# Window attention and maxout FFN on one core: in chunk 1 the mask of head pair 1 becomes a product on VectorE instead of two matmuls, and that pair's value products stand one group of FFN products later

## The chip, the core and the metric

The kernel runs on one core of a Trainium2 chip. The metric is device time in microseconds (us) of one execution. The kernel before takes 177.5 us, the median of 3 runs (177.43 to 177.53).

A core has five engines, each with its own in-order list of instructions; they wait for each other through semaphores. TensorE (PE in the profile) multiplies matrices: it loads a weight block (PEld), streams the other operand past it and writes to PSUM, which has eight banks. VectorE (DVE) and ScalarE (ACT) read PSUM and write SBUF. GpSimd (POOL) works in SBUF only and here also starts the loads of the weights. SyncE's queue (SP) starts the other transfers.

## The reference, cut to what matters

```python
# q, k, v: (4 batches, 8 heads, 768 positions, 64); n_sink 4, window 128
scores = scale * np.matmul(q, k.transpose(0, 1, 3, 2))
rel = pos[:, None] - pos[None, :]
keep = (pos[None, :] < n_sink) | ((rel >= 0) & (rel < window))
a = softmax(np.where(keep, scores, -1e9))
x = np.matmul(a, v)                     # heads put side by side: (3072, 512)
h = np.maximum(np.maximum(x @ w1, x @ w2), x @ w3)      # (3072, 768)
out = h @ w_out                                          # (3072, 512)
```

Inputs and output are float32; the kernel multiplies in bf16 and sums in float32.

## The kernel before, in words

The 3072 tokens are cut into 12 chunks of 256 (three to a batch). Heads go in four pairs, 0 to 3. Every chunk passes through the same steps, each a small function; the order in which their calls are written is the order in which each engine meets its instructions. No scheduler changes it.

- `score(ci, p)`: for one head pair, products of keys and queries (line 287) into two banks named `st`, one for each head of the pair. The window needs four 128x128 blocks per head in a chunk that is not the first of its batch.
- The mask comes in one of two ways. With `premask(ci, p)` ahead of the score, TensorE writes an additive mask (0 or a large negative number) into the two banks, one 128x512 product of the identity and `addm` for each (line 269), and the scores are added onto it; it takes the two banks that early. Without it the scores overwrite the banks, and after the exponential `mask(ci, p)` multiplies both heads' weights by a 0/1 mask in one VectorE instruction of 128x1024 (line 341).
- `expo(ci, p)`: the exponential on ScalarE, one instruction per head (line 335), from `st` to `e_sb`. It sets the two banks free.
- `sink_score` and `av_open`: scores of the four sink positions (line 349), their exponential (line 355), and then the first products into four banks named `o`, one per pair (line 381).
- `av(ci, p)`: the value products of one pair, eight in a chunk like chunk 1 (line 398, output `o`). VectorE then takes the reciprocal of the sums (line 403) and writes the normalised rows to `x_sb` (line 406), which frees the pair's `o` bank.
- `xpose(ci, t, nc.vector)`: four transposes on TensorE into a bank `xt` (line 419) and a copy on VectorE to `xT` (line 420), for each half t of the chunk.
- `ffn_h(ci, fp, wi)`: eight products of `xT` with two of the six column blocks of weight wi (line 438) into one bank `h_ps`. For wi = 0 ScalarE copies the result to `h_sb` (line 445); for wi = 1 and 2 VectorE takes the maximum of it and `h_sb` (line 449). Each of the eight products reads both halves of `xT`.
- `ffn_y(ci, t)`: the output products and their copy.

Banks are handed out from a list, first freed, first given, in the order in which the calls are written. So a call that takes banks earlier or later also changes which bank later calls get, and so for whom they wait.

The change lies in a prologue that is written out call by call, for chunks 0 to 3. Around it stand: scores of chunk 1, pair by pair (0, 2, 3, then 1); the first FFN group of chunk 0, `ffn_h(0, 2, 0)`; the value products of chunk 1; the other FFN groups of chunk 0; the transposes of chunk 1; and then the FFN groups of chunk 1, beginning with `ffn_h(1, 0, 0)`. The weights of the FFN come in parts while this runs, by loads from GpSimd's queue.

Of the kernel before, what the change touches and what calls it, by code (L numbers as in the profile page):

```python
# [16 lines left out]
def kernel(  # L17
# [31 lines left out]
    with tc.manual_schedule():  # L49
# [7 lines left out]
        def bank(shape, dtype, name):  # L57
            j = free.pop(0)
            x = psum.tile(shape, dtype, tag=f"b{j}", name=name)
            home[id(x)] = x, j  # L60
            return x

        def give(*banks):
            for x in banks:
                free.append(home.pop(id(x))[1])
# [10 lines left out]
        def load(ci, what="kqv", gate=None, part=None, parts=1):  # L76
            if ci >= NCH:
                return
            b, c = divmod(ci, CPB)
            t0 = c * 256  # L80
            for w in what:
                src = {"k": k, "q": q, "v": v}[w]
                if (ci, w) not in raws:
                    raws[ci, w] = raw.tile([128, H, 2, D], F32, tag=w + "_raw", name=w + "_raw")
                dst = raws[ci, w]
                if gate is not None:
                    gate(dst[0:1, 0, 0, 0:1])
                n = H // parts
                for g in range(parts) if part is None else (part,):
                    nc.sync.dma_start(  # L90
                        out=dst[:, n * g:n * g + n],
                        in_=src[b, n * g:n * g + n, t0:t0 + 256]
                            .rearrange("h (p i) d -> p h (i d)", i=2))
# [162 lines left out]
        def load_wo(a, b):  # L256
            nc.gpsimd.dma_start(out=wo[:, a:b],
                                in_=moe_w_out.rearrange("(a p) f -> p a f", p=128)[:, a:b])
# [5 lines left out]
        def premask(ci, pairs):  # L264
            lo = 0 if ci % CPB else 1
            for p in pairs:
                sts[ci, p] = [bank([128, 4, 128], F32, "st") for a in range(2)]
                for a in range(2):
                    nc.tensor.matmul(sts[ci, p][a][:, lo:], lhsT=ident, rhs=addm0 if lo else addm,  # L269
                                     start=True, stop=False, skip_group_check=True)  # L270
# [54 lines left out]
        def weight(ci, p, a, s):  # L325
            if (ci, 0) in packed:
                j, u = unit[p, s]
                return packed[ci, j][0][:, a, u]
            return es[ci, p][0][:, a, s]

        def expo(ci, p):
            lo = 0 if ci % CPB else 1
            e, st = es[ci, p]
            for a in range(2):
                nc.scalar.activation(e[:, a, lo:], st[a][:, lo:], AF.Exp, scale=scale)  # L335
                give(st[a])

        def mask(ci, p, eng=None):
            lo = 0 if ci % CPB else 1
            e = es[ci, p][0]  # L340
            (eng or nc.vector).tensor_mul(e[:, :, lo:], e[:, :, lo:], msk0 if lo else msk)  # L341

        def sink_score(ci):
            b, c = divmod(ci, CPB)
            if c == 0:
                return
            st = bank([128, 2, 128], F32, "sk")
            for p in range(NP):
                nc.tensor.matmul(  # L349
                    st[32 * p:32 * p + 32].rearrange("q n (i r) -> q n i r", i=2),  # L350
                    lhsT=ks[b % 2][:, p],
                    rhs=qT[ci % RING][:, p].rearrange("q i n r -> q n i r"),
                    start=True, stop=True, tile_position=(0, 32 * p))
            e = work.tile([128, 2, 128], BF16, tag="e_sink", bufs=2, name="e_sink")
            nc.scalar.activation(e, st, AF.Exp, scale=scale)  # L355
            give(st)
            es[ci, "sink"] = e
# [30 lines left out]
        def av(ci, p):  # L388
            b, c = divmod(ci, CPB)
            o = os_[ci, p]  # L390
            first = c == 0
            for t in range(2):
                for a in range(2):
                    blocks = [(1, ci, 0)] if t == 0 else [(2, ci, 0), (3, ci, 1)]
                    if t == 0 and c:
                        blocks = [(0, ci - 1, 1)] + blocks
                    for s, cv, n in blocks:
                        nc.tensor.matmul(  # L398
                            o[:, t, a], lhsT=weight(ci, p, a, s), rhs=vb[cv % RING][:, n, 2 * p + a],
                            start=first, stop=True, skip_group_check=True)  # L400
                        first = False
            rc = work.tile([128, 2, 2], F32, tag="rc", bufs=4, name="rc")
            nc.vector.reciprocal(rc, o[:, :, :, D])  # L403
            if ci not in xs:
                xs[ci] = work.tile([128, 2, NP, 2, D], BF16, tag="x", bufs=2, name="x_sb")
            nc.vector.tensor_mul(xs[ci][:, :, p], o[:, :, :, 0:D],  # L406
                                 rc.unsqueeze(3).to_broadcast([128, 2, 2, D]))
            give(o)
# [3 lines left out]
        def xpose(ci, t, eng=None):  # L412
            eng = eng or nc.scalar
            if ci not in xTs:
                xTs[ci] = work.tile([128, 2, DS, 128], BF16, tag="xT", bufs=3, name="xT")
            pt = bank([128, DS, 128], BF16, "xt")
            x = xs[ci][:, t].rearrange("q p a d -> q (p a d)")
            for ds in range(DS):
                nc.tensor.transpose(pt[:, ds], x[:, ds * 128:(ds + 1) * 128], ident)  # L419
            (nc.scalar.copy if eng is nc.scalar else eng.tensor_copy)(xTs[ci][:, t], pt)  # L420
            give(pt)
# [9 lines left out]
        def ffn_h(ci, fp, wi, cuts=1):  # L431
            if ci not in hs:
                hs[ci] = work.tile([128, FB, 256], BF16, tag="h", bufs=3, name="h_sb")
            hp = bank([128, 2, 256], F32, "h_ps")
            for f in range(2):
                c0 = (2 * fp + f) * 128
                for ds in range(DS):
                    nc.tensor.matmul(  # L438
                        hp[:, f].rearrange("q (i t r) -> q i t r", i=2, t=2),
                        lhsT=w_sb[wi][:, ds, c0:c0 + 128],  # L440
                        rhs=xTs[ci][:, :, ds].rearrange("q t (i r) -> q i t r", i=2),
                        start=(ds == 0), stop=(ds == DS - 1))
            dst = hs[ci][:, 2 * fp:2 * fp + 2]
            if wi == 0:
                nc.scalar.copy(dst, hp)  # L445
            else:
                for f in range(cuts):
                    x = slice(2 * f // cuts, 2 * (f + 1) // cuts)
                    nc.vector.tensor_max(dst[:, x], dst[:, x], hp[:, x])  # L449
            give(hp)  # L450
# [36 lines left out]
        def after(wi, c=0):  # L487

            def gate(dst):
                nc.gpsimd.tensor_copy(dst, w_sb[wi][0:1, 0, c:c + 1])  # L490
            return gate
# [78 lines left out]
        score(1, (3,))  # L570
        load_w(2, 512, 768)
        sink_score(1)
        premask(1, (1,))
        load(2, 'q', gate=pool_gate)
        cast_v(1, 1, 0, nc.gpsimd)
        load_w(2, 0, 256)
# [10 lines left out]
        av(1, 0)  # L587
        expo(1, 1)
        av(1, 3)
        av(1, 2)  # L590
        ffn_h(0, 1, 0)
        av(1, 1)
        ffn_h(0, 0, 0)
        load_wo(0, 3)
        xpose(1, 0, nc.vector)
        xpose(1, 1, nc.vector)
        load(3, 'k', gate=after(1))
        ffn_h(0, 2, 1)
        ffn_h(1, 0, 0)
        ffn_h(1, 2, 0)  # L600
        ffn_h(1, 1, 0)
# [341 lines left out]
```

## Time and profile before

| what | value |
|---|---|
| median of 3 runs | 177.5 us (177.43 to 177.53) |
| the profiled execution's own time | 177.67 us |
| span, first to last instruction, of that execution | 175.9 us |
| mean granted TensorE clock | 1.000 |
| DVE busy | 125.7 us (71%) |
| ACT busy | 86.0 us (49%) |
| POOL busy | 66.4 us (38%) |
| HBM read and written | 25.17 MB and 6.29 MB |

The span is what the trace shows; the time of the execution holds 1.77 us more that lie around it. Times in the trace count from the span's start. "Busy" of TensorE counts overlapping products once, and the end of a product is modelled: a 128x256 product is shown with 273 ns, though the next one starts 0.11 us after it. Starts are therefore the better measure of TensorE's pace. A bracket behind a row names the idle time just before it and what ended it; small waits carry none.

### The profile page before, as it was taken

How to read it: one execution, taken by the hardware profiler on the slowest of the kernel's cores; microseconds unless marked ns; L12 is line 12 of the kernel's file. 1: busy time of each engine (PE TensorE's matmuls, PEld its weight loads, DVE VectorE, ACT ScalarE, POOL GpSimd, SP SyncE). 2: the span in 40 equal slices, each digit the busy share in tenths (PEclk: the TensorE clock that was granted, in tenths of full speed). 3: DMA queues.
4: the chain of work that ended last, by engine and by line, in shares of the span. 5: the costliest groups of instructions: out<-in, count | busy, mean ns of one | idle time of the engine just before them, and what ended most of it. 6: DMA issues, size and time to landing. Idle time of an engine off the chain costs nothing.

```text
span 175.9 us, 4628 instructions
## 1 busy us (share of the span) xinstructions
PE 169.1 (96%) x1869; PEld 127.4 (72%) x1869; DVE 125.7 (71%) x267; ACT 86.0 (49%) x168; POOL 66.4 (38%) x128
## 2 busy tenths in 40 slices
PE   7789999999999999999999999999999999999991
PEld 2447889856896697697796796796895895896870
DVE  3499728697899687875875975977775875976550
ACT  3479831557847833914716815815517617510211
POOL 4799045146671828035525425326537000000000
PEclk9999999999999999999999999999999999999999
DMA  4999999999979496699999999999999429323203
GB/s 136 292 289 204 208 219 265 238 281 273 261 123 276 77 303 128 120 305 124 207 279 193 197 301 166 235 297 132 198 298 195 150 49 373 120 54 129 121 0 119
DMA packets 69573, 34.90 MB, mean 198 GB/s; under 512 B 26544, under 2 KB 68016, under 8 KB 69552
## 3 DMA queue, kind: packets, MB, share of 16 engines
q1 hardware_dynamic: 64912, 31.33, 78.5%
q0 software_dynamic: 4496, 3.15, 11.7%
q8 instruction: 14, 0.23, 0.6%
q10 hardware_dynamic: 144, 0.13, 0.2%
q14 instruction: 7, 0.06, 0.1%
HBM read 25.17 MB, written 6.29 MB: 179 GB/s over the span
## 4 chain that ended last, share of the span: by engine, by line
PE 91%; DMA 3%; DVE 3%; issue 0%; POOL 0%; ACT 0%; POOLq 0%
PE h_ps L438 54%; PE y_ps L459 18%; PE o L398 6%; PE st L287 6%; DMA q_raw<-in_q_dram 3%; DVE vb L108 2%; PE pt L118 1%; PE xt L419 1%; PE o L381 1%; PE sk L349 1%; PE st L307 1%; PE y_ps L469 1%; PE pt L140 1%; PE st L269 1%; DVE qT L122 0%; DVE k_bf L102 0%
## 5 line engine op out<-in xcount | busy, mean ns | idle before, releaser
L438 PE MATMUL h_ps<-xT,w 128*128 128x256 bf16 x864 | 100.7, 273 | 0.0
L438 PEld LDWEIGHTS <-w 128*128 128x128 bf16 x864 | 82.1, 98 | 10.1 <-issue 0.2
L449 DVE TENSOR_TENSOR h_sb<-h_sb,h_ps 128x512 bf16<-128x512 bf16 (+1 forms) x74 | 49.0, 670 | 18.7 <-PE h_ps L438 17.4
L445 ACT CAST h_sb<-h_ps 128x512 bf16<-128x512 f32 x36 | 21.2, 594 | 45.5 <-PE h_ps L438 45.5
L335 ACT ACTIVATE e_sb<-st 128x512 bf16<-128x512 f32 (+1 forms) x80 | 40.2, 594 | 3.3 <-PE st L287 2.0
L108 POOL CAST vb<-v_raw 64x512 bf16<-64x512 f32 x40 | 27.5, 688 | 13.5 <-DMA v_raw<-in_v_dram 12.1
L459 PE MATMUL y_ps<-wo,h_sb 128*128 128x512 bf16 x138 | 32.2, 380 | 0.0
L341 DVE TENSOR_TENSOR e_sb<-e_sb,msk 128x1024 bf16<-128x1024 bf16 (+1 forms) x34 | 25.1, 764 | 3.8 <-ACT e_sb L335 3.7
L102 POOL CAST k_bf<-k_raw 128x512 bf16<-128x512 f32 x19 | 11.2, 613 | 36.5 <-DMA k_raw<-in_k_dram 33.3
L459 PEld LDWEIGHTS <-h_sb 128*128 128x128 bf16 x138 | 12.5, 98 | 14.8 <-issue 1.2
L406 DVE TENSOR_TENSOR x_sb<-o,rc 128x256 bf16<-128x256 f32 x48 | 20.4, 424 | 1.7
L398 PE MATMUL o<-vb,e_sb 128*128 128x65 bf16 x352 | 16.7, 193 | 0.7 <-DVE vb L108 0.7
L398 PEld LDWEIGHTS <-e_sb 128*128 128x128 bf16 x352 | 14.9, 97 | 3.1 <-issue 0.7
L461 DVE COPY y_sb<-y_ps 128x512 f32<-128x512 f32 x12 | 8.3, 691 | 10.6 <-PE y_ps L459 10.5
L102 POOL CAST q_bf<-q_raw 128x512 bf16<-128x512 f32 x19 | 11.3, 617 | 9.5 <-DMA q_raw<-in_q_dram 9.3
L287 PE MATMUL st<-qT,kT 64*128 64x128 bf16 (+1 forms) x224 | 12.5, 237 | 0.5 <-DVE qT L122 0.5
L287 PEld LDWEIGHTS <-kT 64*128 64x128 bf16 x224 | 7.3, 94 | 5.8 <-issue 4.3
L403 DVE RECIPROCAL rc<-o 128x4 f32<-128x4 f32 x48 | 8.3, 174 | 3.5 <-PE o L398 3.4
L355 ACT ACTIVATE e_sink<-sk 128x256 bf16<-128x256 f32 x8 | 3.1, 390 | 14.2 <-PE sk L349 9.7
L318 ACT ACTIVATE e_sb<-st 128x512 bf16<-128x512 f32 x12 | 6.1, 615 | 4.7 <-PE st L307 4.7
L461 ACT COPY y_sb<-y_ps 128x512 f32<-128x512 f32 x11 | 6.5, 588 | 3.8 <-PE y_ps L459 3.4
L180 PE MATMUL warm<-wz 128*128 128x512 bf16 x11 | 4.9, 632 | 1.2 <-DVE wz L169 1.2
(77 smaller groups left out, 86.4 us busy)
## 6 DMA issues: line engine op xcount, KB each, us to landing
k_raw<-in_k_dram SPq DMA_DIRECT2D x12, 512.0 KB, 6.2
q_raw<-in_q_dram SPq DMA_DIRECT2D x12, 512.0 KB, 7.3
v_raw<-in_v_dram SPq DMA_DIRECT2D x12, 512.0 KB, 7.8
out_dram<-y_sb SPq DMA_DIRECT2D x11, 512.0 KB, 3.9
w<-in_moe_w_dram POOLq DMA_DIRECT2D x5, 256.0 KB, 8.1
w<-in_moe_w_dram POOLq DMA_DIRECT2D x2, 512.0 KB, 9.0
wo<-in_moe_w_out_dram POOLq DMA_DIRECT2D x2, 384.0 KB, 9.2
kT<-k_bf SPq DMA_TRANSPOSE x16, 3.4
```

The lines of the kernel that those rows point to most:

```text
L102: f(x[:, 2 * g:2 * g + 2].rearrange("q p i a d -> q p a i d"), y[:, 4 * g:4 * g + 4].rearrange("q (p a) i d -> q p a i d", a=2))
L108: (eng.copy if eng is nc.scalar else eng.tensor_copy)(vb[ci % RING][64 * i:64 * i + 64, n, :, 0:D], raws[ci, "v"][64 * n:64 * n + 64, :, i])
L287: nc.tensor.matmul(st[a][:, s:s + q1 - q0].rearrange("q n (i r) -> q n i r", i=2), lhsT=x[hp, n, p].rearrange("q i r -> q (i r)"), rhs=qc[ ...
L335: nc.scalar.activation(e[:, a, lo:], st[a][:, lo:], AF.Exp, scale=scale)
L341: (eng or nc.vector).tensor_mul(e[:, :, lo:], e[:, :, lo:], msk0 if lo else msk)
L398: nc.tensor.matmul(o[:, t, a], lhsT=weight(ci, p, a, s), rhs=vb[cv % RING][:, n, 2 * p + a], start=first, stop=True, skip_group_check=True)
L406: nc.vector.tensor_mul(xs[ci][:, :, p], o[:, :, :, 0:D], rc.unsqueeze(3).to_broadcast([128, 2, 2, D]))
L438: nc.tensor.matmul(hp[:, f].rearrange("q (i t r) -> q i t r", i=2, t=2), lhsT=w_sb[wi][:, ds, c0:c0 + 128], rhs=xTs[ci][:, :, ds].rearrang ...
L445: nc.scalar.copy(dst, hp)
L449: nc.vector.tensor_max(dst[:, x], dst[:, x], hp[:, x])
L459: nc.tensor.matmul(yp, lhsT=hs[ci][:, fb, t * 128:(t + 1) * 128], rhs=wo[:, fb], start=(fb == 0), stop=(fb == FB - 1))
L461: (nc.scalar.copy if eng is None else eng.tensor_copy)(ys[ci][:, t], yp)
```

## The change

```diff
         score(1, (3,))
         load_w(2, 512, 768)
         sink_score(1)
-        premask(1, (1,))
         load(2, 'q', gate=pool_gate)
...
         ffn_h(0, 2, 0)
         score(1, (1,))
         av_open(1)
         av(1, 0)
         expo(1, 1)
         av(1, 3)
+        mask(1, 1)
         av(1, 2)
         ffn_h(0, 1, 0)
+        ffn_h(0, 0, 0)
         av(1, 1)
-        ffn_h(0, 0, 0)
         load_wo(0, 3)
+        ffn_h(0, 2, 1)
         xpose(1, 0, nc.vector)
         xpose(1, 1, nc.vector)
         load(3, 'k', gate=after(1))
-        ffn_h(0, 2, 1)
         ffn_h(1, 0, 0)
```

The additive mask of pair 1 is gone, and with it two 128x512 products; `score(1, 1)` now takes its two banks itself, behind `ffn_h(0, 2, 0)`, and its products start fresh instead of adding. One product on VectorE masks the weights after the exponential. `av(1, 1)` changes places with `ffn_h(0, 0, 0)`, and the two transposes of chunk 1 change places with `ffn_h(0, 2, 1)`.

The instructions of ScalarE, GpSimd and SyncE's queue stand in the same order as before. On TensorE, behind the sink scores of chunk 1 (`sk`), the two products that write the mask (`addm` by the identity, to `st`) are gone, and FFN products follow at once:

```order
 L349 MATMUL sk<-qT_74,ks_81 32x256
-L269 LDWEIGHTS ident
-L269 MATMUL st<-addm,ident 128x512
-L269 LDWEIGHTS ident
-L269 MATMUL st<-addm,ident 128x512
 L438 LDWEIGHTS w_104
 L438 MATMUL h_ps<-xT,w_104 128x256
```

What moved: nothing; four instructions are left out. Further on, on TensorE behind the last transpose of chunk 1, the kernel before has this (`xT_338` is the turned x of chunk 0, `w1` the second FFN weight):

```order
L419 LDWEIGHTS x_sb_444
L419 MATMUL xt_509<-ident_93,x_sb_444 128x128
L438 LDWEIGHTS w1_105 [waits DMASW2_49]
L438 MATMUL h_ps_518<-xT_338,w1_105 128x256
```

And the changed kernel, at the same place (`xT_511` is the turned x of chunk 1, `w0` the first weight):

```order
L419 LDWEIGHTS x_sb_442
L419 MATMUL xt_518<-ident_93,x_sb_442 128x128
L438 LDWEIGHTS w0_104
L438 MATMUL h_ps_528<-xT_511,w0_104 128x256 [waits DVE_49]
```

What moved: the eight products of `ffn_h(0, 2, 1)`, which read chunk 0, went ahead of the transposes; the product behind the transposes is now the first that reads chunk 1, and it waits for VectorE. On VectorE, from the normalisation of pair 3 of chunk 1 (`rc`, `x_sb`) to its first products of the FFN (`h_sb`):

```order
 L403 RECIPROCAL rc<-o 128x4
 L406 TENSOR_TENSOR x_sb<-o,rc 128x2x128
-L403 RECIPROCAL rc<-o 128x4
-L406 TENSOR_TENSOR x_sb<-o,rc 128x2x128
-L403 RECIPROCAL rc<-o 128x4
-L406 TENSOR_TENSOR x_sb<-o,rc 128x2x128
+L341 TENSOR_TENSOR e_sb<-e_sb,msk 128x1024
+L403 RECIPROCAL rc<-o 128x4
+L406 TENSOR_TENSOR x_sb<-o,rc 128x2x128
+L403 RECIPROCAL rc<-o 128x4
+L406 TENSOR_TENSOR x_sb<-o,rc 128x2x128
+L449 TENSOR_TENSOR h_sb<-h_sb,h_ps 128x512
```

What moved: the new product of the mask stands between the normalisations of pairs 3 and 2, and one maximum of the FFN, which stood behind the copies of `xT`, now stands ahead of them.

## The prediction

> **What bounds the kernel now.** I read the page's busy times first, then the chain of waits, then the stretch of the change on each engine. The page says that TensorE carries nearly the whole span, and the table by stretches says more: from 22.51 us, where the changed part ends, to 171.5 us it is never idle.
>
> ```profile
> PE 169.1 (96%) x1869; PEld 127.4 (72%) x1869; DVE 125.7 (71%) x267; ACT 86.0 (49%) x168; POOL 66.4 (38%) x128
> 16.49:22.51 6.02, 6.02 (x89) 4.90 (x88) 4.76 (x13) 4.65 (x10) 1.22 (x3) 1.00 1.28 208
> 22.51:171.50 148.99, 148.99 (x1649) 114.99 (x1647) 109.83 (x221) 70.73 (x138) 52.37 (x91) 1.00 0.90 197
> ```
>
> In the last two rows the second and third numbers count: length of the stretch and TensorE's busy time in it, 148.99 of 148.99 us. So nothing behind the change can swallow a delay, and nothing can hide a gain: what the changed stretch takes longer or shorter comes out at the end one to one. The question is when the first product of `ffn_h(1, 0, 0)` starts, since from there both kernels have the same TensorE work in the same order.
>
> Here is TensorE in that stretch (start, length, instruction; count at the end):
>
> ```profile
> 16.16 0.29 PE L349 MATMUL sk<-qT,ks 128*32 128x256 bf16 x4
> 16.49 0.38 PE L269 MATMUL st<-addm,ident 128*128 128x512 bf16 x1
> 16.70 0.38 PE L269 MATMUL st<-addm,ident 128*128 128x512 bf16 x1
> 16.92 1.03 PE L438 MATMUL h_ps<-xT,w 128*128 128x256 bf16 x8
> 17.89 0.39 PE L287 MATMUL st<-qT,kT 64*128 64x128 bf16 x6
> 18.21 0.29 PE L381 MATMUL o<-vs,e_sink 32*128 32x130 bf16 x8
> 18.44 0.90 PE L398 MATMUL o<-vb,e_sb 128*128 128x65 bf16 x24
> 19.18 1.03 PE L438 MATMUL h_ps<-xT,w 128*128 128x256 bf16 x8
> 20.05 0.40 PE L398 MATMUL o<-vb,e_sb 128*128 128x65 bf16 x8
> 20.29 1.04 PE L438 MATMUL h_ps<-xT,w 128*128 128x256 bf16 x8
> 21.16 0.64 PE L419 MATMUL xt<-ident,x_sb 128*128 128x128 bf16 x8
> 21.64 8.02 PE L438 MATMUL h_ps<-xT,w 128*128 128x256 bf16 x72
> ```
>
> By starts, a group of eight FFN products takes 0.87 us (19.18 to 20.05), eight value products 0.24 (20.05 to 20.29), eight transposes 0.48 (21.16 to 21.64). The last row holds `ffn_h(0, 2, 1)` and then `ffn_h(1, 0, 0)`, so the latter starts at 21.64 + 0.87 = 22.51.
>
> **The change part by part.** *The two mask products go.* They hold TensorE from 16.49 to 16.92, 0.43 us. The FFN group behind them needs both copies of `xT` of chunk 0; the second ends at 16.43, and the mask product waited for the same copy, since it got the bank from which it was made. So the group can start at 16.49, and the whole 0.43 is saved: -0.43.
>
> ```profile
> 16.02 0.41 DVE L420 COPY xT<-xt 128x512 bf16<-128x512 bf16 x1
> 17.09 0.43 ACT L355 ACTIVATE e_sink<-sk 128x256 bf16<-128x256 f32 x1
> 17.35 0.66 ACT L335 ACTIVATE e_sb<-st 128x512 bf16<-128x512 f32 x1
> 17.83 0.67 ACT L335 ACTIVATE e_sb<-st 128x512 bf16<-128x512 f32 x1
> 18.31 0.67 ACT L445 CAST h_sb<-h_ps 128x512 bf16<-128x512 f32 x1
> 19.26 0.71 ACT L335 ACTIVATE e_sb<-st 128x512 bf16<-128x512 f32 x1
> ```
>
> From 16.43 to 16.49 lie 0.06 us between VectorE's end and TensorE's start; I use that for every hand-over.
>
> *Part of it is lost at once.* ScalarE does not come forward: its instructions follow each other without a hole up to 19.97 (19.26 + 0.71, the end of pair 1's exponential). The sink products of `av_open` fill four banks, and the fourth, pair 3's, is the one that the first exponential of pair 3 gives back at 17.35 + 0.66 = 18.01. TensorE would be at the sink products at 18.21 - 0.43 = 17.78, and must wait for the fourth until 18.07; the value products, 0.22 behind the fourth (18.44 less 18.22), start at 18.29 instead of 18.01. That costs +0.28. It costs 0 if that wait falls away, which is the low bound. The second exponential of pair 3 ends at 18.50 and is wanted at 18.29 + 0.24 + 0.06 = 18.59, so nothing more is lost there.
>
> *The product on VectorE.* It waits for the exponential's end at 19.97 and starts at 20.03. VectorE is free by then: pair 0's and pair 3's normalisations move up with TensorE (from 18.89 to 18.74, at 0.55 each: done at about 19.9).
>
> ```profile
> 16.47 0.93 DVE L341 TENSOR_TENSOR e_sb<-e_sb,msk 128x1024 bf16<-128x1024 bf16 x1
> 17.68 0.67 DVE L341 TENSOR_TENSOR e_sb<-e_sb,msk 128x1024 bf16<-128x1024 bf16 x1
> 18.89 0.18 DVE L403 RECIPROCAL rc<-o 128x4 f32<-128x4 f32 x1 [0.54 <-PE o L398]
> 19.45 0.17 DVE L403 RECIPROCAL rc<-o 128x4 f32<-128x4 f32 x1
> 16.24 0.61 POOL L108 CAST vb<-v_raw 64x512 bf16<-64x512 f32 x1
> 18.95 0.18 POOL L490 CAST k_raw<-w 1x1 f32<-1x1 bf16 x1 [1.42 <-DMA w<-in_moe_w_dram]
> 23.34 0.17 POOL L490 CAST v_raw<-w 1x1 f32<-1x1 bf16 x1 [4.21 <-DMA w<-in_moe_w_dram]
> ```
>
> The same instruction took 0.93 us while a GpSimd cast ran (16.24 to 16.85) and 0.67 when none did. From 19.13 to 23.34 GpSimd stands still, so I take 0.67: the masked weights are there at 20.70, for TensorE at 20.76. TensorE has then done `ffn_h(0, 1, 0)` from 19.18 - 0.43 + 0.28 = 19.03 and `ffn_h(0, 0, 0)`, and comes to `av(1, 1)` at 20.77. The moved group covers the product to within 0.01 us: 0. With 0.93 instead it would be +0.25, the high bound. The Trainium skill, "SBUF — State Buffer", "Who interferes with whom", says that a VectorE instruction with two SBUF inputs and a GpSimd instruction that reads SBUF exclude each other. The trace agrees (0.93 against 0.67), and by that rule too the product here meets nobody and costs 0.67.
>
> Queued behind the product on VectorE are the normalisations of pairs 2 and 1: 20.65, 21.20, done at about 21.8. The transpose that reads pair 1 comes at about 21.96. No loss, with 0.15 to spare.
>
> *The moved transposes.* TensorE goes from `av(1, 1)` (20.78 to 21.02) to `ffn_h(0, 2, 1)` (to 21.89) and the transposes (to 22.37). Its weights are there: that part of `w1` was issued at 12.75 and landed 7.1 us later, at about 19.9.
>
> ```profile
> 12.75 1.48 POOL L251 DMA_DIRECT2D w<-in_moe_w_dram  x2
> w<-in_moe_w_dram POOLq DMA_DIRECT2D x1, 256.0 KB, 7.1
> ```
>
> Then comes `ffn_h(1, 0, 0)`, every product of which reads both halves of `xT`, and so waits for both copies. Before, `ffn_h(0, 2, 1)` stood between and covered them:
>
> ```profile
> 21.61 0.76 DVE L420 COPY xT<-xt 128x512 bf16<-128x512 bf16 x2 [0.44 <-PE xt L419]
> 21.95 0.41 DVE L420 COPY xT<-xt 128x512 bf16<-128x512 bf16 x1
> 22.78 0.69 DVE L449 TENSOR_TENSOR h_sb<-h_sb,h_ps 128x512 bf16<-128x512 bf16 x1 [0.41 <-PE h_ps L438]
> 31.67 0.69 DVE L449 TENSOR_TENSOR h_sb<-h_sb,h_ps 128x512 bf16<-128x512 bf16 x1 [0.18 <-PE h_ps L438]
> 32.27 0.42 DVE L125 COPY kT<-pt 128x512 bf16<-128x512 bf16 x1
> ```
>
> Copies alone: from the first transpose (21.16) to the end of the second copy (21.95 + 0.41 = 22.36) is 1.20, with the hand-over 1.26, of which the transposes fill 0.48. That would be a hole of 0.78. But in VectorE's new order the maximum of `ffn_h(0, 2, 1)` stands ahead of the copies. It starts 1.14 after that group's first product (21.64 to 22.78), here at 21.02 + 1.14 = 22.16. The next VectorE instruction follows 0.60 later (31.67 to 32.27): the first copy at 22.76, the second at 23.10 (0.34 on, as 21.61 to 21.95), its end at 23.51, TensorE at 23.57. The hole is 23.57 - 22.37 = 1.20 us: +1.20.
>
> **Sum.** -0.43 + 0.28 + 0 + 1.20 = +1.05 us; `ffn_h(1, 0, 0)` starts at about 23.56 instead of 22.51. The profiled execution would go from a span of 175.9 to 176.95 and, with the 1.77 around it, from 177.67 to 178.72. That execution lies 0.17 above the median, so against the median I predict 177.5 + 1.05 = **178.55 us**. Bounds: low with a hole of 0.78 and no loss at the sink products, -0.43 + 0.78 = +0.35; high with the contended product, 1.05 + 0.25 = +1.30, and 0.15 more if the hand-overs are slower.
>
> **The rivals.** *The copies do not hold TensorE* (faster). Place: between the last transpose and `ffn_h(1, 0, 0)`. If those products could begin on what is there, only the first two terms stand: -0.43 + 0.28 = -0.15, 177.35 us, or 177.07 if the sink products lose nothing. It decides from a hole below 0.15. For it: TensorE's small waits often show no bracket. Against: the first product of that group carries a wait for VectorE, and the wait of 16.43 to 16.49 shows that such waits are kept. 3%.
>
> *The maximum does not delay the copies.* It would have to be shorter or sooner than its rows say. Then the hole is 0.78: +0.35 to +0.63, 177.85 to 178.13 us. Against: the maximum cannot start before its group ends, and VectorE keeps its order. 8%.
>
> *The product is stretched*: GpSimd works at 20.0 after all. +1.30, 178.8 us. Against: its rows above. 5%.
>
> *The hole slows TensorE's clock.* The first products of the kernel, 128x512 like the mask products, took 632 ns against 378, while the granted clock read 1.00:
>
> ```profile
> L180 PE MATMUL warm<-wz 128*128 128x512 bf16 x11 | 4.9, 632 | 1.2 <-DVE wz L169 1.2
> L269 PE MATMUL st<-addm,ident 128*128 128x512 bf16 x4 | 1.2, 378 | 0.0
> 11.63 0.25 PE L398 MATMUL o<-vb,e_sb 128*128 128x65 bf16 x3 [0.65 <-DVE vb L108]
> ```
>
> Those 11 took 4.87 us, 0.42 apart where the mask products are 0.21 apart. If the hole brought that back for as long, about 2.4 us would be lost on top: 181 us. Against: idle times up to 0.65 us (last row) left the following products as quick as others. 2%. The Trainium skill, "TensorE: Matmul & The Clock Gate", "Why this matters for your kernels", allows gaps up to about 3 us before the clock falls. By that rule a hole of 1.2 us costs itself alone; no run here shows a longer one once the array is warm.
>
> **How the numbers follow.** Chances: the forecast 82%, the rivals 3, 8, 5 and 2. The forecast's spread is its unknown terms; with the second and third rivals the range is 177.95 to 179.0. A measurement tells about 0.2% (0.36 us) from no change here. Faster than that needs the first rival: 4% with what I may have missed. Within it lies the lowest end of the second rival: 6%. Slower: 90%.
>
> **What would show it.** Right: TensorE's two 128x512 mask products gone and the FFN group at 16.5; the sink products held to about 18.1; a VectorE product near 20.0 of about 0.67 us; the value products of pair 1 at 20.8 with hardly a wait; copies of `xT` near 22.8 and 23.1; an idle time of about 1.2 us before an FFN product at 23.5, and the same pace behind it. Wrong: no such hole, copies ahead of the maximum, a stretched product, FFN products behind the hole farther apart than 0.11 us, or idle time of TensorE gone from somewhere behind 23.6.

## The result, and the profile after

The changed kernel takes 178.43 us (median of 6 runs, 178.17 to 179.01) against 177.39 us for the kernel before (177.17 to 177.53, 6 runs): 1.0064 times as long, 95% interval 1.0038 to 1.0089. That is 1.04 us slower; 1.05 was forecast. The six runs of the changed kernel lie in two groups, 178.17 to 178.26 and 178.60 to 179.01, and their median falls between them. The profiled execution took 178.87.

The page of the changed kernel's profiled execution, its busy times, and the table by stretches with the same columns as before (stretch; length; busy time of PE, PEld, DVE, ACT, POOL):

```profile
PE 167.8 (95%) x1867; PEld 126.7 (72%) x1867; DVE 127.0 (72%) x268; ACT 86.0 (49%) x168; POOL 66.2 (37%) x128
22.51:23.56 1.05, 0.08 (x2) 0.00 (x0) 1.03 (x3) 0.00 (x0) 0.17 (x1) 1.00 1.28 213
23.56:172.50 148.94, 148.77 (x1645) 114.71 (x1645) 109.62 (x220) 70.63 (x137) 52.06 (x90) 1.00 0.90 195
```

TensorE is busy for 1.3 us less than before and the span is 1.2 us longer (177.1). The 1.3 us are not the change: all of them lie in the first 10 us, ahead of it, where TensorE's first products were shorter in this execution (busy 6.58 us there, 7.88 before). The work that the edit takes away is two products. Between 22.51 and 23.56 us TensorE is idle but for the drain of its last product, while VectorE works through all of it. Here are TensorE's and VectorE's instructions there, in order of time (start, length, instruction, count):

```profile
16.26 0.29 PE L349 MATMUL sk<-qT,ks 128*32 128x256 bf16 x4
16.59 1.03 PE L438 MATMUL h_ps<-xT,w 128*128 128x256 bf16 x8
17.55 0.40 PE L287 MATMUL st<-qT,kT 64*128 64x128 bf16 x6
17.88 0.56 PE L381 MATMUL o<-vs,e_sink 32*128 32x130 bf16 x8
18.37 0.90 PE L398 MATMUL o<-vb,e_sb 128*128 128x65 bf16 x24
19.11 1.91 PE L438 MATMUL h_ps<-xT,w 128*128 128x256 bf16 x16
20.86 0.42 PE L398 MATMUL o<-vb,e_sb 128*128 128x65 bf16 x8
21.11 1.04 PE L438 MATMUL h_ps<-xT,w 128*128 128x256 bf16 x8
21.98 0.61 PE L419 MATMUL xt<-ident,x_sb 128*128 128x128 bf16 x8
23.59 7.15 PE L438 MATMUL h_ps<-xT,w 128*128 128x256 bf16 x64 [1.00 <-DVE xT L420]
```

```profile
20.11 0.69 DVE L341 TENSOR_TENSOR e_sb<-e_sb,msk 128x1024 bf16<-128x1024 bf16 x1
21.53 0.42 DVE L406 TENSOR_TENSOR x_sb<-o,rc 128x256 bf16<-128x256 f32 x1
22.18 0.69 DVE L449 TENSOR_TENSOR h_sb<-h_sb,h_ps 128x512 bf16<-128x512 bf16 x1 [0.23 <-PE h_ps L438]
22.79 0.75 DVE L420 COPY xT<-xt 128x512 bf16<-128x512 bf16 x2
```

The reader is to see three things. The sink products (L381), eight of them, are stretched from 0.29 to 0.56 us: by the forecast's account they wait inside for the fourth bank. The value products of pair 1 start at 20.86, 0.06 after the product on VectorE ends (20.11 + 0.69) and 1.75 after the two FFN groups begin, which is what two groups take: nobody waits long for the other. And the FFN products of chunk 1 begin at 23.59 with a bracket of 1.00 for VectorE's copies, which stand behind the maximum. The chain of waits (start, length, what) says the same:

```profile
21.27 0.89 PE h_ps L438 x8
22.16 0.02 issue
22.18 0.69 DVE h_sb L449
22.87 0.68 DVE xT L420 x2
23.55 0.04 issue
23.59 6.49 PE h_ps L438 x58
```

This execution started 0.10 us later than the one profiled before: the first sink score stands at 16.26 instead of 16.16. So from here on I count from that score (line 349) to the first FFN product of chunk 1: 22.51 - 16.16 = 6.35 us before, 23.59 - 16.26 = 7.33 in the changed kernel, 0.98 more.

### The profile page after: what moved, and what is told of

Read it like the earlier page. It is cut to its first block, busy times and chain, and to the rows that moved or that the text cites. A ratio compares the mean times of both kernels' runs of the same rounds, so it can differ in the third digit from the quotient of the medians.

```text
span 177.1 us, 4624 instructions
## 1 busy us (share of the span) xinstructions
PE 167.8 (95%) x1867; PEld 126.7 (72%) x1867; DVE 127.0 (72%) x268; ACT 86.0 (49%) x168; POOL 66.2 (37%) x128
## 3 DMA queue, kind: packets, MB, share of 16 engines
q0 software_dynamic: 4496, 3.15, 11.6%
## 4 chain that ended last, share of the span: by engine, by line
PE 86%; DVE 6%; DMA 3%; ACT 2%; issue 1%; POOL 0%; POOLq 0%
PE h_ps L438 51%; PE y_ps L459 17%; PE o L398 6%; PE st L287 5%; DMA q_raw<-in_q_dram 3%; DVE vb L108 2%; DVE h_sb L449 2%; ACT e_sb L335 1%; PE pt L118 1%; PE o L381 1%; PE st L307 1%; PE sk L349 1%; PE y_ps L469 1%; PE pt L140 1%; DVE x_sb L406 1%
## 5 line engine op out<-in xcount | busy, mean ns | idle before, releaser
L341 DVE TENSOR_TENSOR e_sb<-e_sb,msk 128x1024 bf16<-128x1024 bf16 (+1 forms) x35 | 26.2, 775 | 3.0 <-ACT e_sb L335 2.7
L102 POOL CAST k_bf<-k_raw 128x512 bf16<-128x512 f32 x19 | 11.9, 650 | 38.9 <-DMA k_raw<-in_k_dram 36.2
L323 DVE TENSOR_TENSOR e_sb<-e_sb,mskp 128x1024 bf16<-128x1024 bf16 x6 | 4.5, 744 | 1.5 <-ACT e_sb L318 1.5
```

The lines of the kernel that those rows point to most:

```text
L102: f(x[:, 2 * g:2 * g + 2].rearrange("q p i a d -> q p a i d"), y[:, 4 * g:4 * g + 4].rearrange("q (p a) i d -> q p a i d", a=2))
```

## The experiments

The theory: TensorE loses 1.1 us in the hole before the first FFN product of chunk 1, because the copies of `xT` have lost their cover and stand behind a maximum; the removed products win part of it back; the product on VectorE is hidden, though barely. The rivals: the product or the late value products are the loss; or the copies do not matter. Two distances are read in each profile: from the first sink score to the second FFN group, `ffn_h(0, 1, 0)`, and from there to the first FFN product of chunk 1. Where no hole parts that product from the group ahead of it, its start is the start of their common row and 0.87 us (1.75 and 2.62 in e7 and e11, which issue that group two and three times).

| kernel | score to second group | from there on | sum, us | median, us | ratio to before (95% interval) |
|---|---|---|---|---|---|
| before | 3.02 | 3.33 | 6.35 | 177.39 | |
| changed | 2.85 | 4.48 | 7.33 | 178.43 | 1.0064 (1.0038 to 1.0089) |
| e1, transposes back | 3.15 | 4.17 | 7.32 | 178.21 | 1.0036 (1.0023 to 1.0048) |
| e2, maximum late | 2.99 | 4.10 | 7.09 | 177.98 | 1.0024 (1.0014 to 1.0033) |
| e3, transposes alone | 3.19 | 4.54 | 7.73 | 178.99 | 1.0072 (1.0050 to 1.0094) |
| e4, mask alone | 3.01 | 4.00 | 7.01 | 178.17 | 1.0029 (1.0017 to 1.0041) |
| e5, values alone | 2.96 | 4.17 | 7.13 | 177.94 | 1.0040 (1.0028 to 1.0052) |
| e6, product twice | 3.09 | 5.02 | 8.11 | 179.18 | 1.0104 (1.0086 to 1.0123) |
| e7, group twice | 3.01 | 4.19 | 7.20 | 178.01 | 1.0056 (1.0034 to 1.0078) |
| e8, sink products split | 3.05 | 4.47 | 7.52 | 178.23 | 1.0056 (1.0039 to 1.0073) |
| e9, no mask of pair 1 | 2.99 | 3.32 | 6.31 | 177.27 | 1.0005 (0.9992 to 1.0019) |
| e10, no product | 3.03 | 4.55 | 7.58 | 178.29 | 1.0061 (1.0049 to 1.0074) |
| e11, group thrice | 3.04 | 5.06 | 8.10 | 179.08 | 1.0096 (1.0083 to 1.0110) |

The ratio compares with runs of the kernel before on the same chip: median 177.57 us beside e1 to e4, 177.24 beside e5 to e8, 177.31 beside e9 to e11.

**e1: the transposes back in their place.** The changed kernel with

```diff
+        xpose(1, 0, nc.vector)
+        xpose(1, 1, nc.vector)
+        load(3, 'k', gate=after(1))
         ffn_h(0, 2, 1)
-        xpose(1, 0, nc.vector)
-        xpose(1, 1, nc.vector)
-        load(3, 'k', gate=after(1))
```

> The changed kernel with the two transposes of chunk 1 ahead of the FFN group (0,2,1) again; mask product and late value products of pair 1 stay. Counted from the first sink score of chunk 1 to the first FFN product of chunk 1 (6.35 us before, 7.33 in the changed kernel). Theory (the hole comes from the copies standing behind the maximum): the copies are covered by the group again, but the transpose of pair 1 now stands 0.9 us nearer to pair 1's normalisation, which ends at 5.69, so a smaller hole opens there: 7.04, that is 0.69 over before, about 178.1 us. Rival (the loss is the product on VectorE and the late value products, not the place of the transposes): no change against the changed kernel, 7.33, 178.4 us. Rival (the copies do not matter at all, only the removed products): below before, 177.0 us.

Measured: from the second group on 4.17 us, where the expectation has 7.04 - 2.85 = 4.19; 0.64 us slower than before. TensorE's rows:

```profile
18.87 1.92 PE L438 MATMUL h_ps<-xT,w 128*128 128x256 bf16 x16 [0.17 <-DMA w<-in_moe_w_dram]
20.87 0.22 PE L419 MATMUL xt<-ident,x_sb 128*128 128x128 bf16 x1
21.77 0.56 PE L419 MATMUL xt<-ident,x_sb 128*128 128x128 bf16 x7 [0.68 <-DVE x_sb L406]
22.17 3.55 PE L438 MATMUL h_ps<-xT,w 128*128 128x256 bf16 x31
```

The hole has moved from behind the transposes to inside them: the second one waits for pair 1's normalisation. The first row shows something that the expectation lacked, a wait for FFN weights ahead of the second group; it is why the sum is 7.32 and not 7.04 (e8 and e9 come back to it). So the sum alone, which the rival put at 7.33, does not tell the two apart; the rows do, and the time, 0.64 over before where the theory had 0.69 and the rival 1.0, stands by the theory.

**e2: the maximum behind the copies.** The changed kernel, with the maximum of the group taken out of its function:

```diff
-        ffn_h(0, 2, 1)
+        ffn_h(0, 2, 1, late=True)     # its products, no maximum
         xpose(1, 0, nc.vector)
         xpose(1, 1, nc.vector)
+        max_late()                    # the maximum, bank given back
```

> The changed kernel with the maximum of the FFN group (0,2,1) behind the two copies on VectorE; TensorE's order as in the changed kernel. Theory (of the hole of 1.13 us the maximum causes the part above the bare copies): first copy as soon as the first transposes are through, a hole of about 0.78 us, first FFN product of chunk 1 at 6.98 after the first sink score (7.33 in the changed kernel, 6.35 before), about 178.05 us. Rival (the maximum does not delay the copies): no change, 7.33, 178.4 us.

Measured: 4.10 from the second group on, where the expectation has 6.98 - 2.85 = 4.13; 0.41 us slower than before. (The sum is 7.09 and not 6.98, again because the second group came late: 2.99 for 2.85.) The first copy starts at once behind the first four transposes, and the bracket shrinks from 1.00 to 0.62:

```profile
22.10 0.76 DVE L420 COPY xT<-xt 128x512 bf16<-128x512 bf16 x2 [0.46 <-PE xt L419]
22.77 0.68 DVE L459 TENSOR_TENSOR h_sb<-h_sb,h_ps 128x512 bf16<-128x512 bf16 x1
22.91 2.78 PE L440 MATMUL h_ps<-xT,w 128*128 128x256 bf16 x24 [0.62 <-DVE xT L420]
```

So the maximum makes 0.38 us of the hole (4.48 - 4.10), and the uncovered copies make the rest.

**e3: the transposes alone.** The kernel before, with only this edit:

```diff
+        ffn_h(0, 2, 1)
         xpose(1, 0, nc.vector)
         xpose(1, 1, nc.vector)
         load(3, 'k', gate=after(1))
-        ffn_h(0, 2, 1)
```

> The kernel before with one edit: the FFN group (0,2,1) ahead of the two transposes of chunk 1. The two mask products stay on TensorE. Theory: nothing is saved and the whole hole opens: first FFN product of chunk 1 at 7.55 after the first sink score (6.35 before), 1.20 over before, about 178.6 us, slower than the changed kernel. Rival (the loss is the product on VectorE): no change against before, 177.4 us.

Measured: 4.54 from the second group on, 1.21 over before, and the hole is there:

```profile
23.71 1.25 PE L438 MATMUL h_ps<-xT,w 128*128 128x256 bf16 x10 [1.07 <-DVE xT L420]
```

The swap of transposes and FFN group makes it without pair 1's product on VectorE. The time missed the expectation: 1.42 us slower, where 1.2 was expected. The sum is 7.73 for 7.55, since the second group came 0.17 later than in the kernel before (3.19 for 3.02), and chunk 3 lost some 0.3 us more, of which the last section tells.

**e4: the mask alone.** The kernel before, with only these:

```diff
-        premask(1, (1,))
...
         av(1, 3)
+        mask(1, 1)
         av(1, 2)
```

> The kernel before with the mask of pair 1 as a product on VectorE instead of the two matmuls; the value products of pair 1 and the transposes stay where they were before. Theory: TensorE comes to the value products of pair 1 at 3.72 after the first sink score, and the masked weights are there at 4.60, so a hole of 0.88 us opens ahead of them and eats more than the 0.43 saved; with 0.26 lost at the sink products the first FFN product of chunk 1 stands at 7.07 (6.35 before), 0.72 over before, about 178.1 us. Rival (the product is free on VectorE and the swaps are the whole loss): 5.92 to 6.18, 177.0 to 177.2 us, faster than before.

Measured: 7.01 where 7.07 was expected; 0.60 us slower. By starts the hole is 0.69 us (18.82 + 0.87 to 20.38) and not 0.88, because the second group came 0.16 later than in the changed kernel; what was lost there was not lost again here. TensorE stands ahead of the value products of pair 1 until the product is done:

```profile
19.63 0.69 DVE L341 TENSOR_TENSOR e_sb<-e_sb,msk 128x1024 bf16<-128x1024 bf16 x1
20.38 0.42 PE L398 MATMUL o<-vb,e_sb 128*128 128x65 bf16 x8 [0.52 <-DVE e_sb L341]
```

**e5: the value products alone.** The kernel before, with only this:

```diff
-        av(1, 1)
         ffn_h(0, 0, 0)
+        av(1, 1)
```

> The kernel before with one edit: the value products of pair 1 stand behind the FFN group (0,0,0) instead of ahead of it. Mask products stay on TensorE, transposes stay ahead of the FFN group (0,2,1). Theory: the transpose of pair 1 follows those value products at once and waits for pair 1's normalisation (reciprocal, then product, about 0.8 us): first FFN product of chunk 1 at 7.14 after the first sink score (6.35 before), 0.79 over before, about 178.2 us. Rival (this swap is free, TensorE has other work): 6.35, 177.4 us.

Measured: 7.13 where 7.14 was expected; 0.70 us slower. Each of the three edits alone costs: 0.60 (e4), 0.70 (e5), 1.42 (e3, the 0.3 of chunk 3 included). All three together cost 1.04, since they cover one another: the swap of the value products hides the product, and the swap of the transposes hides the normalisation that the late value products bring.

**e6: the product twice.** The changed kernel with a second `mask(1, 1)` behind the first.

> The changed kernel with the mask product of pair 1 issued twice (the mask is 0 or 1, the second changes nothing). Theory (the product ends within 0.05 us of the moment at which TensorE wants its result, so it has no slack): the second one, 0.6 us, comes out whole: value products of pair 1 at about 5.2 after the first sink score instead of 4.60, first FFN product of chunk 1 at 7.95 instead of 7.33, about 179.0 us. Rival (VectorE has slack there): less than 0.2 us, 178.4 to 178.6 us.

Measured: 8.11, 0.78 more than the changed kernel (0.54 from the second group on); 1.94 us slower than before, 179.18 us. The extra 0.6 us comes out nearly whole from the second group on; the rest of the 0.78 is a second group that came late (3.09 for 2.85). The product had no slack, as the tie at 20.86 above says.

**e7: TensorE delayed, nothing moved.** The kernel before with `reps=2`, which issues the eight products of `ffn_h(0, 2, 1)` twice.

> The kernel before with the eight products of the FFN group (0,2,1) issued twice into the same bank, nothing moved: 0.87 us more of TensorE work and no new wait. Theory (TensorE sets the end from here on, so a delay comes out one to one): first FFN product of chunk 1 at 7.22 after the first sink score (6.35 before), 178.25 us; a coincidence of VectorE's products with GpSimd's casts around 50 us may add up to 0.3. Rival (a later wait swallows part of it): less than 0.5 us, below 177.9 us.

Measured: 7.20 where 7.22 was expected; 0.77 us slower for 0.87 us of work. A delay comes out, within what these runs resolve: three of the five took 177.92 to 178.01 us, two 178.70 and 178.81.

**e8: the sink products split.** The changed kernel, with `av_open` in two steps:

```diff
-        av_open(1)
+        av_open(1, (0, 1, 2))
         av(1, 0)
+        av_open(1, (3,))
```

> The changed kernel with the sink products of pair 3, which wait for a bank that ScalarE gives back, behind the value products of pair 0 instead of ahead of them. Theory A (the 0.26 us lost at the sink products is a term of the sum): TensorE's value products of pair 0 start 0.26 us sooner, part of it lost again at pair 3, and the first FFN product of chunk 1 comes up to 0.26 sooner than 7.33 after the first sink score, 178.2 us. Theory B (the mask product sets the start of pair 1's value products anyway, at 4.60, since ScalarE ends the exponential when it does): the value products of pair 0 come sooner, those of pair 1 do not, 7.33 stays, 178.4 us.

Measured: neither. The value products of pair 0 do start sooner, 1.76 us after the first sink score for 2.11 in the changed kernel, so a part of the sink products did wait. But TensorE gains ahead of the second FFN group and then loses it there: its value products of pairs 3 and 2 are done at 18.06 + 0.49 = 18.55 (the pace of the other rows), but the group starts at 18.79.

```profile
17.50 0.42 PE L399 MATMUL o<-vb,e_sb 128*128 128x65 bf16 x8
18.06 0.66 PE L399 MATMUL o<-vb,e_sb 128*128 128x65 bf16 x16
18.79 1.92 PE L439 MATMUL h_ps<-xT,w 128*128 128x256 bf16 x16
18.79 0.18 POOL L491 CAST k_raw<-w 1x1 f32<-1x1 bf16 x1 [1.01 <-DMA w<-in_moe_w_dram]
PEld L439 <- DMA w<-in_moe_w_dram: 0.2, 1, 0.2
```

GpSimd's small cast waits for the same part of `w0`, and is released in the same moment; the last row, of the view of waits, names the load. This execution reached the sink scores at 15.74, half a microsecond before the profiled executions of the two kernels (16.16 and 16.26), and so ran into weights that land at about 18.75. Which of its two theories holds is left open by this run: the weights stand in front of both.

**e9: the removed products priced alone.** The kernel before without `premask(1, (1,))`, nothing in its place.

> The kernel before without the two mask products of pair 1 of chunk 1 and with nothing in their place: that pair's mask is left out. Nothing is moved. It prices the removed products by themselves. Theory (the forecast's terms, 0.43 saved and 0.26 lost again since ScalarE is not sooner, and in executions that start early the FFN weights of group (0,1,0) land at about 18.75 us and take more of it): the second FFN group starts at most 0.17 us sooner, value products of pair 1 wait up to 0.15 for their exponential, so first FFN product of chunk 1 between 6.2 and 6.4 after the first sink score (6.35 before), 0 to 0.15 us faster, 177.2 to 177.4. Rival (the products cost TensorE 0.43 us on the path): 5.92, 0.43 us faster, about 176.9.

Measured: 6.31 (6.35 before), ratio 1.0005 with an interval from 0.9992 to 1.0019: no change. TensorE's 0.43 us go to the waits for ScalarE's bank and for the weights:

```profile
17.38 0.61 PE L381 MATMUL o<-vs,e_sink 32*128 32x130 bf16 x8
17.92 0.90 PE L398 MATMUL o<-vb,e_sb 128*128 128x65 bf16 x24
18.84 1.05 PE L438 MATMUL h_ps<-xT,w 128*128 128x256 bf16 x8
```

The sink products take 0.61 instead of 0.29, and the FFN group starts at 18.84 though the value products need only 0.74 from 17.92 on. (At 37.9 us TensorE waited 1.09 us for a part of the output weights, a wait that no other profile has there; behind it nothing of this profile is read. Two of the eleven runs took 178.37 and 178.45 us, the profiled one being the latter, the other nine 177.03 to 177.63.)

**e10: the changed kernel without the product.** Both swaps stay, `mask(1, 1)` is gone.

> The changed kernel without the product on VectorE (that pair's mask is left out); both swaps stay. Theory (the moved FFN group covers the product to within 0.05 us; the loss is the hole before the first FFN product of chunk 1, which the maximum ahead of the copies makes): value products of pair 1 and the hole stand as in the changed kernel, first FFN product of chunk 1 at 4.48 after the second FFN group's first product, the same as the changed kernel within 0.05, 178.3 us. Rival (the product on VectorE is what costs): back to 177.4 to 177.7 us.

Measured: 4.55 from the second group on against 4.48, ratio 1.0061 against the changed kernel's 1.0064. Without the product the kernel is as slow as with it, and the hole is there:

```profile
23.24 0.92 PE L438 MATMUL h_ps<-xT,w 128*128 128x256 bf16 x7 [1.07 <-DVE xT L420]
```

**e11: the group three times.** As e7, with `reps=3`.

> The kernel before with the eight products of the FFN group (0,2,1) issued three times, nothing moved: 1.75 us more of TensorE work. Theory (chunk 3's mask products on VectorE take 2.85 us for three when the first starts later than about 47.7 us, where they meet GpSimd's casts, whose time the loads set; they took 0.55, 0.57 and 0.7 when it starts earlier): first mask product of chunk 3 at about 48.0, three in about 2.9 us, idle TensorE of about 0.3 us ahead of the transposes of chunk 3, and 1.75 + 0.3 over before, 179.3 us. Rival (a delay comes out one to one): products of 0.55 to 0.8 us each, 1.75 over before, 179.0 us.

Measured: 1.77 us slower than before for 1.75 us of work: one to one, as the rival said. The products on VectorE were stretched, as the theory said (2.43 us for three), but TensorE hardly waited for them (0.1 us in chunk 3's transposes). The last section says more.

None of these kernels is faster than the kernel before. With the two mask products gone and nothing in their place there is nothing to win (e9), so no place for a product on VectorE can make this edit pay while the rest of the order stays as it is.

## Why the prediction was right

The time came out at 178.43 us for 178.55, and the mechanism is the one that was forecast: each term can be read in the profiles of the two kernels. That the difference agrees to 0.01 us is in part luck. The median lies between two groups of runs, of which the lower is 0.8 us slower than before and the higher about 1.5. Behind the change, too, the profiled executions show a gain of 0.17 and a loss of 0.31 us that the forecast did not have.

- *The two mask products go, -0.43.* From the first sink score to the first FFN group: 0.76 us before (16.92 - 16.16), 0.33 in the changed kernel (16.59 - 16.26). -0.43, as forecast.
- *Part of it is lost at once, +0.28.* Score to value products: 2.28 before (18.44 - 16.16), 2.11 in the changed kernel (18.37 - 16.26). So 0.26 of the 0.43 was lost, at the sink products.
- *The product on VectorE, 0.* It took 0.69 us (0.67 forecast), ended at 20.80, and TensorE took its result at 20.86 with both groups just done. e10 and e6 bear this out from both sides: without it nothing is won, and twice it costs. Behind it pair 1's normalisation ended at 21.95 (21.53 + 0.42), where about 21.8 was forecast, so the 0.15 that the forecast had to spare there was all but used up.
- *The hole, +1.20.* From the last transpose (21.98 + 0.48 = 22.46, the transposes at the pace of before) to 23.59: 1.13. e2 parts it into the maximum's share, 0.38, and the copies' share.
- *Sum.* -0.43 + 0.26 + 1.13, and 0.02 at the value products of pair 1, is the 0.98 read above. With the 0.10 of the later start it makes 1.08 at the first FFN product of chunk 1 (23.59 against 22.51). From there to chunk 3's transposes 0.17 of it was swallowed: they begin 0.91 later (55.55 against 54.64). In them 0.31 was added (0.92 us for 0.61), which gives the span's 1.2.

Two sentences of the prediction hold less firmly than they were put. "Nothing behind the change can swallow a delay, and nothing can hide a gain" rests on a busy time of 148.99 in 148.99 us, and a short wait can hide in a row that counts as busy. Here are a mask product on VectorE and the value products on TensorE behind it, first before, then in the changed kernel:

```profile
41.02 1.07 DVE L341 TENSOR_TENSOR e_sb<-e_sb,msk 128x1024 bf16<-128x1024 bf16 x1
41.56 1.01 PE L398 MATMUL o<-vb,e_sb 128*128 128x65 bf16 x24
42.06 0.68 DVE L341 TENSOR_TENSOR e_sb<-e_sb,msk 128x1024 bf16<-128x1024 bf16 x1
42.60 0.89 PE L398 MATMUL o<-vb,e_sb 128*128 128x65 bf16 x24
```

GpSimd casts from 40.39 to about 41.55 in both. In the kernel before the product runs beside the casts and ends at 42.09, while the value products are under way, and they take 0.12 us longer; in the changed kernel it comes behind the casts and is short. So the kernel before held a small wait here, which the delay removed. Over whole runs e7 and e11 give 0.77 for 0.87 and 1.77 for 1.75: a delay comes out, but only within some 0.3 us either way.

The other is the saving of 0.43. In the changed kernel's profile -0.17 of it is left behind ScalarE. But the profiles of all eleven experiments reach the first sink score 0.18 to 0.50 us sooner than that of the kernel before, and in ten of them the second FFN group starts at 18.65 to 18.87 us, with the mask products (e5, e7, e11) or without, near the landing of its weights. The prediction looked at the landing of `w1` and not at that of `w0`, on which this group rests. e9 prices the two terms, forecast together at -0.15, over eleven runs: nothing, within -0.14 to +0.34 us. How much of them the changed kernel's runs without a profile keep is open.

Of the rivals, "the copies do not hold TensorE" falls with e3 and the bracket of 1.00, "the maximum does not delay the copies" with e2, "the product is stretched" with its 0.69 us. The clock did not fall: the 64 products behind the hole take 7.15 us, 0.109 us apart by starts ((7.15 - 0.27) / 63), as before the hole.

## What to carry to other kernels

Taking work from the engine that bounds the kernel is worth only what the next wait leaves of it: before counting the saving, look at what that engine needs next (here a bank that ScalarE gives back, then weights), and when it gets it. Work that stands between a producer and its consumer on the bounding engine is cover; whoever moves a group out of such a gap has to price the whole way that it covered, transposes, the copies, and whatever has slipped ahead of the copies on their engine. Edits of an order are not additive: here three of them, each a loss, together lose less than their sum, so each has to be walked through with the others in place.

## What the runs showed that was not expected

VectorE's three first mask products of chunk 3 (128x768) come in two forms. In the kernel before they took 0.55, 0.56 and 0.80 us, with waits for ScalarE between; in the changed kernel the three stand back to back and take 2.85:

```profile
46.88 0.55 DVE L341 TENSOR_TENSOR e_sb<-e_sb,msk 128x768 bf16<-128x768 bf16 x1
47.95 0.56 DVE L341 TENSOR_TENSOR e_sb<-e_sb,msk 128x768 bf16<-128x768 bf16 x1 [0.52 <-ACT e_sb L335]
48.71 0.80 DVE L341 TENSOR_TENSOR e_sb<-e_sb,msk 128x768 bf16<-128x768 bf16 x1 [0.21 <-ACT e_sb L335]
```

```profile
47.75 2.85 DVE L341 TENSOR_TENSOR e_sb<-e_sb,msk 128x768 bf16<-128x768 bf16 x3
47.63 0.68 POOL L108 CAST vb<-v_raw 64x512 bf16<-64x512 f32 x1 [1.58 <-DMA v_raw<-in_v_dram]
55.55 0.92 PE L419 MATMUL xt<-ident,x_sb 128*128 128x128 bf16 x8
```

GpSimd's casts start when a load lands, at 47.45 and 47.63 us in the two kernels. When VectorE's first product is begun before, it goes through; when it comes behind the cast, all three take longer. It was 2.85 us in the changed kernel, e3 and e6, whose first product starts at 47.75 to 47.97, and short in e1 (47.45), e8 (47.42) and e10 (47.39). In the changed kernel the transposes of chunk 3 then take 0.92 us instead of 0.61, 0.3 us of TensorE; the row of before is this:

```profile
54.64 0.61 PE L419 MATMUL xt<-ident,x_sb 128*128 128x128 bf16 x8
```

So a delay of 1 us can turn a meeting of two other engines, 25 us later, from harmless into one that costs. That this splits the changed kernel's six runs (178.17 to 178.26, and 178.60 to 179.01) is likely but not shown, since only one of them has a profile, 178.87 us, of the higher group. e8 and e10, with the same hole and the short form, took 178.22 and 178.25 us in their profiled executions, as the lower group did. And e11, meant to show the cost, met the casts later, at 48.42, and lost little.
